# Another order for the first four chunks: scores of the second chunk ahead of the first y, six w_in pieces ahead of the third chunk's products

## The chip, the cores and the metric

The kernel runs on one core of a Trainium2 chip. The time is the device time of one execution in microseconds (us); before the change it is the median of three runs. Five engines work side by side, each through its own list of instructions in order: TensorE (PE, with its weight loads shown as PEld), VectorE (DVE), ScalarE (ACT), GpSimd (POOL) and SyncE (SP, which here issues the loads). They wait for each other through semaphores.

## The reference

A gated linear attention recurrence over 768 tokens (4 batches, 8 heads, 48 numbers a head) is followed by a feed-forward layer with SiLU on its 3072 rows of 384:

```python
for t in range(S):
    state = alpha[:, :, t, :, None] * state + np.einsum('bhd,bhe->bhde', k[:, :, t], v[:, :, t])
    y[:, :, t] = np.einsum('bhd,bhde->bhe', q[:, :, t], state)
x = y.transpose(0, 2, 1, 3).reshape(B * S, H * D)
h = x @ w_in                               # w_in 384 x 2048
out = (h * (1.0 / (1.0 + np.exp(-h)))) @ w_out   # w_out 2048 x 384
```

The weights w_in and w_out reach the kernel as 8-byte floats and are turned to 4-byte floats on the chip.

## The kernel before, in words

**Chunks.** The tokens are cut into 24 chunks of 128 (six for each batch; chunk n belongs to batch n mod 4). The recurrence of a chunk is done with matmuls. Four stages do it, each a function of the chunk's number:

- `products(n)`: PE transposes a (alpha), k and q; ACT copies a to SBUF (L731). DVE makes u, the products of alpha toward the chunk's end (a scan, L734), then kp = k times u (L745), then by `quotient(n)` the running products p (a scan, L764) and qp = q times p (L770). Below, these six DVE instructions are the chunk's DVE chain.
- `scores(n)`: PE multiplies kp with qp; ACT copies the two halves of the scores to g (L812), POOL sets what lies above the diagonal to zero (L813). PE transposes kp, and ACT copies that as kn (L832).
- `values(n)`: PE multiplies v with the masked scores (and the state with qp, from chunk 4 on), which is y; ACT copies y into `xt` (L863). One `xt` holds two chunks.
- `states(n)`: PE multiplies v with kn; ACT copies it as the state of a batch (L882), later DVE adds it.

**Feed-forward.** `enter_plain` multiplies an `xt` of two chunks with w_in, two tiles of 128 columns at a time: six matmuls and a SiLU on ACT (L923) are one step. `leave` multiplies with w_out. These steps stand in the list `pieces` and are dealt out between the stages by `fill`.

**Weights.** `weights` converts w_in in twelve pieces of 128 x 512 and then w_out in sixteen. For each piece ACT rounds the low words (`up`, L629) and DVE takes three instructions (L645, L646, L647). Raw bits lie in four buffers, and `fetch` loads the next piece once the buffer of the piece four before it has been read. `up` has two buffers. Pieces 0 to 2 are needed for the first four tiles of columns, 3 to 5 for the next four, and so on.

**Order.** The loop over `step` runs the four stages of neighbouring chunks, and after each stage (a slot) `fill` is called: up to `marks[0]`, at slot 10, it converts pieces of w_in (three of them), afterwards it gives out feed-forward steps as they fall due, with conversions ahead of them. Loads are issued in the same order on SP: `load(n)` brings a, k and q of a chunk, `load_v(n)` its v. Buffers for a, k and q exist twice, for kn and the scores g once, and PSUM has three banks (`ps_a`) in turn for transposes, scores, y and states. A planner orders the instructions of each engine unless they are held by `tc.keep_in_program_order`; `in_order` does that for PE's matmuls only from the time `late` is filled, some chunks further on. With both kernels the built program states each engine's list.

Of the kernel before, what the change touches and what calls it, by code (L numbers as in the profile page):

```python
# [8 lines left out]
F32 = mybir.dt.float32  # L9
# [4 lines left out]
ALU = mybir.AluOpType  # L14
# [341 lines left out]
def quotients(  # L356
# [22 lines left out]
    late = {}  # L379

    def in_order(ins):

        return tc.keep_in_program_order(ins) if late else ins

    class pe:
        @staticmethod
# [8 lines left out]
    C = 128  # L395
# [218 lines left out]
    def weights(which):  # L614

        pieces = [
            (w_in[:, t, c : c + 512], moe_w_in[t * 128 : t * 128 + 128, c : c + 512])  # L620
            for t, c in pieces_in
        ] if which == 0 else [
            (w_out[:, f, :], moe_w_out[f * 128 : f * 128 + 128, :]) for f in range(NFT)]
        def rounding(bits):
            n = bits.shape[1]
            up = upp.tile([128, 512], I32, name="up")[:, 0:n]

            tc.keep_in_program_order(
                act.activation(up, bits.bitcast(U32)[:, :, 0], AF.Copy, scale=2.0**-29))  # L629
            return up  # L630

        ahead = []
        for i, (dst, src) in enumerate(pieces):
            if not wide:
                act.dma_start(dst, src)
                yield
                continue
            assert which == 0 or conv_done[0] == n_conv[0]
            bits = coming.pop(0)
            up = ahead.pop() if ahead else rounding(bits)  # L640
            if which == i == 0:
                yield
            hi, w = bits[:, :, 1], dst.bitcast(I32)
            tc.keep_in_program_order(
                dve.tensor_scalar(w, hi, 3, 0x3FFFFFFF, ALU.logical_shift_left, ALU.bitwise_and))  # L645
            dve.scalar_tensor_tensor(w, hi, -(1 << 30), w, ALU.bitwise_and, ALU.bitwise_or)  # L646
            dve.tensor_tensor(w, w, up, ALU.add)  # L647
# [62 lines left out]
    def products(n):  # L710

        c = ctxs[n]
        sg = seg[0 if late else n % 2]
        ps = {}

        for name in ("a", "k", "q"):
            if n >= NA:
                if name == "a":
                    turned(c[name], tokens(sg))
                    load(n + 1, "a")  # L720
                continue
            if n < GB and name != "a":

                at = "kq".index(name)
                ps[name] = (bank(at) if n == 1 else out_bank(at, 512)).rearrange("p (j c) -> p j c", c=C)
            else:
                ps[name] = ps_attn()
            for j in range(NP):
                pe.transpose(ps[name][:, j, :], c[name][:, 2 * j : 2 * j + 2, :], ident)
            if name == "a":  # L730
                act.copy(tokens(sg), ps[name])  # L731
        end = NP * W
        u = upool.tile([128, end + 1], F32, name="u")
        dve.tensor_tensor_scan(u[:, end - 1 :: -1], sg[:, end:0:-1], one[:, end:0:-1],  # L734
                               0.0, ALU.mult, ALU.add)

        dve.tensor_single_scalar(least[:, n, :], u[:, 0:end:W], 2.0**-64, ALU.max)
        kp = c["kp"] = turns(kps, n) if n < NA else kps[0]
        ut = tokens(u)
        if n >= NA:  # L740
            ps["k"] = late["turn"].tile([128, NP, C], F32, name="turn")
            turned(c["k"], ps["k"])
            load(n + 1, "k")
        if n < NA:
            dve.tensor_tensor(kp, ps["k"], ut, ALU.mult)  # L745
            quotient(n, sg, ps["q"])
            return
        j = NP // 2
        dve.tensor_tensor(kp[:, 0:j], ps["k"][:, 0:j], ut[:, 0:j], ALU.mult)
        k, ut = [x[:, j:].rearrange("p j (e c) -> p j e c", e=2) for x in (ps["k"], ut)]  # L750
        dve.tensor_tensor(kp[:, j:].rearrange("p j (e c) -> p j e c", e=2)[:, :, ::-1], k, ut, ALU.mult)
        c["sg"] = sg

    def quotient(n, sg=None, q=None):

        c = ctxs[n]
        if sg is None:
            if n < NA:
                return
            sg = c.pop("sg")  # L760
        end, iv = NP * W, inv
        dve.reciprocal(iv[:, 0:end:W], least[:, n, :])
        p = turns(qps if n < NA else [qps[0], late["p"]], n)
        dve.tensor_tensor_scan(p[:, 0:end], sg[:, 0:end], iv[:, 0:end], 0.0, ALU.mult, ALU.add)  # L764
# [5 lines left out]
        dve.tensor_tensor(qp, q, qp, ALU.mult)  # L770

    def flip(n):

# [18 lines left out]
    def scores(n):  # L792
        c = ctxs[n]
        ci, b = c["ci"], c["b"]
        ps = [ps_attn() for _ in range(2)]

        for j in (0, 2, 1, 3):
            for e in range(2 if n >= NA else 1):  # L800
                for u in range(2):
                    r = slice(64 * u, 64 * u + D)
                    at = slice(CH * e, CH * e + CH) if n >= NA else slice(0, C)
                    t = slice(CH * (e ^ j // 2) if n >= NA else 0, C)
                    pe.matmul(ps[u][at, j, t], lhsT=c["kp"][r, j, at], rhs=c["qp"][r, j, t],
                              start=True, stop=True)
        g = decayed.rearrange("p (u j c) -> p u j c", u=2, j=NP)
        swapped = decayed.rearrange("p (o u j c) -> p o u j c", o=2, u=2, j=NP // 2)
        c["g"] = (lambda u, j: g[:, u, j, :]) if n < NA else (
            lambda u, j: swapped[:, j // 2, u, j % 2, :])  # L810
        for u in range(2 if n < NA else 0):
            act.copy(g[:, u], ps[u])  # L812
            gps.affine_select(g[:, u], g[:, u], pattern=[[0, NP], [1, C]], compare_op=ALU.is_ge,  # L813
                              fill=0.0, base=0, channel_multiplier=-1)
        if n >= NA:
            ps = [x.rearrange("p (o j) c -> p o j c", o=2) for x in ps]
            for u in range(2):
                act.copy(swapped[:, :, u, :, CH:], ps[u][:, :, :, CH:])  # L818
            for r, o in earlier:
                for u in range(2):  # L820
                    act.copy(swapped[r, o, u, :, 0:CH], ps[u][r, o, :, 0:CH])
            for at, half in ((CH, later), (0, earlier)):
                for r, o in half:
                    x = swapped[r, o].rearrange("p u j c -> p (u j) c")[:, :, at : at + CH]
                    gps.affine_select(x, x, pattern=[[0, NP], [1, CH]],  # L825
                                      compare_op=ALU.is_ge, fill=0.0, base=0, channel_multiplier=-1)
        if n < NA and ci < NCH - 1:
            ps_k = ps_attn()
            for j in range(NP):
                pe.transpose(ps_k[:, j, :], c["kp"][:, j, :], ident)  # L830
            c["kn"] = work.tile([128, NP, C], F32, name="kn")
            act.copy(c["kn"], ps_k)  # L832
        if ci > 0:
            s = st[b].rearrange("p j u e -> p j (u e)")
            for j in range(NP):
                mul = act.mul(s[:, j], s[:, j], least[:, n, j : j + 1])
                if late:
                    tc.keep_in_program_order(mul)
# [345 lines left out]
    def fill(step, slot):  # L1184

        at = step * SLOTS + slot
        if at < marks[0]:
            if at == SLOTS:
                next(conv[0])
            elif step >= 1:  # L1190
                convert(0, (at - SLOTS) * 3 // (marks[0] - SLOTS) + 1)
            return
        i = next(i for i, m in enumerate(marks[1:]) if at < m)
        a, b = [work_at[n] for n in ([0] + phases)[i : i + 2]]
        due = a + (b - a) * (at - marks[i] + 1) / (marks[i + 1] - marks[i])
        if at % 2 == 0 and step > 3 * GB + 2:
            next(audits, None)
        while work_at[done + 1] <= due and pieces[done][2] <= bridged:
# [2 lines left out]
            go_on()  # L1201

    for step in range(STEPS):
        if step == 1:
            load(NIN)
        stages = [[(scores, 1)], [(products, 0)], [(values, 1)], [(states, 1)]]
        if step == 1:

            stages = stages[1::-1] + stages[2:]
        elif step >= NA:  # L1210
            stages = [[(land, 1), (scores, 1)], [(products, 0)], [(quotient, 0)],
                      [(values, 1), (states, 1), (flip, 0)]]
        for slot, group in enumerate(stages):
            for stage, lag in group:
# [99 lines left out]
```

## Time and profile before

| | us |
|---|---|
| median of three runs | 557.77 (557.57 to 557.89) |
| the profiled execution | 557.26 |
| its span, first to last instruction | 555.5 |
| PE busy in the span | 541.4 |
| DVE busy in the span | 445.4 |
| ACT busy in the span | 208.5 |

The span is counted from the program's first instruction; a moment in the trace is given in us from there. A line of the timeline gives the start, the duration, the engine, the line of the kernel, the operation, what it writes and reads, and in square brackets the idle time before it and what ended it. Matmul counts in the trace are those of records: a 4-byte matmul of the program is mostly two of them.

### The profile page before, as it was taken

Reading aid. Unit: us, or ns where it says so; the run is one execution under the profiler, and the core shown is the slowest. Engines: PE = TensorE matmul, PEld = TensorE weight load, DVE = VectorE, ACT = ScalarE, POOL = GpSimd, SP = SyncE. Lnnn points to the kernel's source line nnn. Section 1 sums busy time; section 2 is a strip of 40 time slices with the busy share of each in tenths; the row PEclk is TensorE's granted clock in tenths of the full one; section 3 lists DMA queues with packets and bytes.
Section 4 is the critical chain, followed back from the end, with each engine's and each line's share of the span. In section 5 each row is a group of like instructions: output and inputs, shape, how many; then the busy total and the mean of one; then the engine's idle time right before and its main releaser. Section 6 shows DMA issues by size and latency. Waiting matters only on the chain. (4 is left out here: it accounts for less than half of the span.)

```text
span 555.5 us, 12640 instructions
## 1 busy us (share of the span) xinstructions
PE 541.4 (97%) x5026; PEld 489.7 (88%) x5026; DVE 445.4 (80%) x801; ACT 208.5 (38%) x466; POOL 76.1 (14%) x146
## 2 busy tenths in 40 slices
PE   6999999999999999999999999999999999999996
PEld 4788887998899999899999999988998999999996
DVE  5897788974999899997998986998884796945431
ACT  2556653223333253353353353344263342332100
POOL 3210000222210212021011021021121000001000
PEclk9999999999999999999999999999999999999999
DMA  9998971164454625355545654617642135500000
GB/s 215 246 249 210 232 195 33 47 161 116 117 136 125 159 63 138 86 145 149 139 112 139 193 139 120 191 27 183 170 137 91 54 91 169 172 11 22 10 24 30
DMA packets 99217, 70.09 MB, mean 126 GB/s; under 512 B 56272, under 2 KB 88656, under 8 KB 99152
## 3 DMA queue, kind: packets, MB, share of 16 engines
q1 hardware_dynamic: 97232, 65.30, 45.1%
q0 software_dynamic: 1920, 3.93, 2.0%
q8 instruction: 40, 0.66, 0.5%
q14 instruction: 25, 0.20, 0.1%
HBM read 61.34 MB, written 7.86 MB: 125 GB/s over the span
## 5 line engine op out<-in xcount | busy, mean ns | idle before, releaser
L388 PE MATMUL ps_o<-w_out,g 128*128 128x192 f32 x768 | 134.0, 328 | 0.5 <-DVE o L1056 0.5
L388 PEld LDWEIGHTS ps_o<-w_out,g 128*128 128x128 f32 x768 | 125.6, 190 | 3.5 <-DVE o L1056 1.0
L388 PE MATMUL ps_m<-xt,w_in 128*128 128x256 f32 x480 | 113.6, 383 | 1.5 <-ACT xt L863 1.1
L388 PEld LDWEIGHTS ps_m<-xt,w_in 128*128 128x128 f32 x480 | 89.1, 190 | 14.4 <-ACT xt L863 1.6
L388 PE MATMUL ps_o<-wt,g 128*128 128x192 f32 x576 | 99.7, 326 | 0.0
L388 PEld LDWEIGHTS ps_o<-wt,g 128*128 128x128 f32 x576 | 95.1, 190 | 1.6 <-issue 0.2
L388 PE MATMUL ps_m<-xc,w_in 128*128 128x256 f32 x288 | 70.7, 382 | 0.0
L388 PEld LDWEIGHTS ps_m<-xc,w_in 128*128 128x128 f32 x288 | 53.7, 190 | 7.0 <-DVE g L958 0.3
L1047 DVE TENSOR_TENSOR g<-g 128x512 f32<-128x512 f32 x72 | 50.1, 709 | 8.3 <-PE ps_o L388 8.3
L955 ACT ACTIVATE g<-g 128x1024 f32<-128x1024 f32 x32 | 33.1, 1056 | 61.2 <-DVE g L958 61.1
L1059 POOL DMA_DIRECT2D out_dram<-o x40 | 22.0, 551 | 219.5 <-DVE o L1056 113.7
L825 POOL TENSOR_SCALAR_AFFINE_SELECT g<-g 64x256 f32<-64x256 f32 x64 | 34.9, 546 | 124.4 <-ACT g L818 105.7
L388 PE MATMUL ps_m<-xc,wx 128*128 128x256 f32 x192 | 50.1, 383 | 1.0 <-DVE xc L586 1.0
L950 ACT COPY g<-ps_m 128x512 f32<-128x512 f32 x64 | 36.6, 588 | 37.0 <-PE ps_m L388 36.9
L388 PEld LDWEIGHTS ps_m<-xc,wx 128*128 128x128 f32 x192 | 35.2, 190 | 5.2 <-ACT u L1078 1.2
L958 DVE TENSOR_TENSOR g<-ps_m,g 128x512 f32<-128x512 f32 x56 | 37.1, 683 | 3.2 <-PE ps_m L388 2.7
L734 DVE TENSOR_TENSOR_SCAN u<-al,one 128x516 f32<-128x516 f32 x24 | 29.8, 1240 | 11.9 <-ACT al L731 11.6
L923 ACT ACTIVATE g<-ps_m 128x512 f32<-128x512 f32 x32 | 19.1, 597 | 41.7 <-PE ps_m L388 41.4
L950 ACT COPY part<-ps_m 128x512 f32<-128x512 f32 x32 | 18.9, 590 | 38.0 <-PE ps_m L388 24.0
L697 DVE TENSOR_REDUCE seen<-bits 128x1 f32<-128x512 int32 (+1 forms) x33 | 26.3, 823 | 5.7 <-DMA bits<-in_moe_w_in_dram 5.7
L764 DVE TENSOR_TENSOR_SCAN p<-al,inv 128x516 f32<-128x516 f32 x24 | 29.9, 1247 | 1.0 <-PE ps_a L388 0.3
L1056 DVE TENSOR_TENSOR o<-ps_o,u 128x192 f32<-128x192 f32 x24 | 8.5, 355 | 25.7 <-PE ps_o L388 22.8
(129 smaller groups left out, 648.5 us busy)
## 6 DMA issues: line engine op xcount, KB each, us to landing
bits<-in_moe_w_in_dram SPq DMA_DIRECT2D x24, 512.0 KB, 4.7
bits<-in_moe_w_out_dram SPq DMA_DIRECT2D x16, 384.0 KB, 3.9
at<-in_alpha_dram SPq DMA_DIRECT2D x64, 96.0 KB, 2.5
kt<-in_k_dram SPq DMA_DIRECT2D x64, 96.0 KB, 2.6
qt<-in_q_dram SPq DMA_DIRECT2D x64, 96.0 KB, 2.7
bits<-in_alpha_dram SPq DMA_DIRECT2D x9, 512.0 KB, 4.0
out_dram<-o POOLq DMA_DIRECT2D x40, 96.0 KB, 2.4
flips<-turn SPq DMA_DIRECT2D x12, 256.0 KB, 2.4
```

What stands on the lines that cost most here:

```text
L388: in_order(nc.tensor.matmul(*args, **kw))
L697: dve.tensor_reduce(seen[kind][which][:, i : i + 1], x, axis=AX, op=op, apply_absolute_value=True))
L734: dve.tensor_tensor_scan(u[:, end - 1 :: -1], sg[:, end:0:-1], one[:, end:0:-1], 0.0, ALU.mult, ALU.add)
L764: dve.tensor_tensor_scan(p[:, 0:end], sg[:, 0:end], iv[:, 0:end], 0.0, ALU.mult, ALU.add)
L825: gps.affine_select(x, x, pattern=[[0, NP], [1, CH]], compare_op=ALU.is_ge, fill=0.0, base=0, channel_multiplier=-1)
L923: act.activation(gts[grp, h, pair][:, i : i + 2, q % 2, :], ps, AF.Silu)
L950: act.copy(to, ps)
L955: act.activation(x, x, AF.Silu)
L958: dve.tensor_tensor(to, a, b, op)
L1047: dve.tensor_tensor(cells(grp, h, pair, *to), cells(grp, h, pair, *x), cells(grp, h, pair, *y), ALU.subtract)
L1056: dve.tensor_tensor(o, x, y, ALU.add)
L1059: (gps if grp < NG - 1 else nc.sync).dma_start(out[r : r + C, c * HO : (c + 1) * HO], o)
```

## The change

In `step` 1 the order of the stages becomes: products of chunk 1; scores of chunk 0; then scores of chunk 1 and values of chunk 0; states of chunk 0. In `step` 2 the slots hold nothing, values of chunk 1, states of chunk 1, products of chunk 2, so that the first feed-forward steps and the conversion of pieces 0 to 5 stand ahead of `products(2)`. The scores of chunk 1 and its kn get a place of their own, in one tile of the pool of g tiles. In the first four steps `settled` and `in_order` hold DVE's and PE's instructions in program order. The loads of chunks 2, 3 and 4 get new places among the slots (`load(NIN)`, `load(NIN + 1)`, `load(NIN + 2)` with NIN = 2).

```diff
     def in_order(ins):
-        return tc.keep_in_program_order(ins) if late else ins
+        return tc.keep_in_program_order(ins) if late or stated[0] else ins
+
+    stated = [True]
+
+    def settled(ins):
+
+        return tc.keep_in_program_order(ins) if stated[0] else ins
...
-            dve.scalar_tensor_tensor(w, hi, -(1 << 30), w, ALU.bitwise_and, ALU.bitwise_or)
-            dve.tensor_tensor(w, w, up, ALU.add)
+            settled(
+                dve.scalar_tensor_tensor(w, hi, -(1 << 30), w, ALU.bitwise_and, ALU.bitwise_or))
+            settled(dve.tensor_tensor(w, w, up, ALU.add))
...
-        dve.tensor_tensor(qp, q, qp, ALU.mult)
+        settled(dve.tensor_tensor(qp, q, qp, ALU.mult))
...
-        g = decayed.rearrange("p (u j c) -> p u j c", u=2, j=NP)
+        if n == 1:
+
+            room = gpool.tile([128, 4, 2, TB], F32, name="g").rearrange("p a b n -> p (a b n)")
+        g = (room[:, 0 : 2 * NP * C] if n == 1 else decayed).rearrange(
+            "p (u j c) -> p u j c", u=2, j=NP)
...
-            c["kn"] = work.tile([128, NP, C], F32, name="kn")
+            c["kn"] = room[:, 2 * NP * C :][:, 0 : NP * C].rearrange(
+                "p (j c) -> p j c", j=NP) if n == 1 else work.tile([128, NP, C], F32, name="kn")
...
             elif step >= 1:
-                convert(0, (at - SLOTS) * 3 // (marks[0] - SLOTS) + 1)
+                convert(0, 6 if at + 1 == marks[0] else (at - SLOTS) * 3 // (marks[0] - SLOTS) + 1)
+            if at == SLOTS + 2:
+                load(NIN)
+            if at + 1 == marks[0]:
+                load(NIN + 1)
             return
...
+        if at == 2 * SLOTS + 3:
+            load(NIN + 2)
+        if step == 2:
+            due = work_at[1 if at == marks[0] else 4]
...
     for step in range(STEPS):
-        if step == 1:
-            load(NIN)
+        stated[0] = step < 4
         stages = [[(scores, 1)], [(products, 0)], [(values, 1)], [(states, 1)]]
         if step == 1:
 
-            stages = stages[1::-1] + stages[2:]
+            stages = [[(products, 0)], [(scores, 1)], [(scores, 0), (values, 1)], [(states, 1)]]
+        elif step == 2:
+            stages = [[], [(values, 1)], [(states, 1)], [(products, 0)]]
...
-                if stage is states and n + 1 + NIN < NA:
+                if stage is states and NIN + 2 < n + 1 + NIN < NA:
                     load(n + 1 + NIN)
```

The other instructions of a chunk's DVE chain (u, least, kp, the reciprocal, p) are wrapped in `settled` in the same way. In the built programs the lists of PE, DVE and ACT differ up to the scores and the DVE chain of chunk 3 and are the same from there on, and SP's list is the same from the loads of chunk 4 on.

| order before | order after |
|---|---|
| PE: scores 0, values 0, states 0, scores 1, transposes of chunk 2 among values 1, states 1, w_in step, w_in step, scores 2, w_in step, transposes of chunk 3, w_in step, values 2 | PE: scores 0, scores 1, values 0, states 0, values 1, states 1, w_in step, transposes of chunk 2, three w_in steps, scores 2, transposes of chunk 3, values 2 |
| DVE: chains of chunks 0 and 1, pieces 0 to 2, chain of chunk 2, pieces 3 to 8 (the last inside the chain of chunk 3), pieces 9 to 11 | DVE: chains of chunks 0 and 1, pieces 0 to 5, chain of chunk 2, pieces 6 to 8, chain of chunk 3, pieces 9 to 11 |
| SP: a, k, q of chunk 2, w_in pieces 4 and 5, a, k, q of chunk 3, v of chunk 2, pieces 6 to 9 | SP: a of chunk 2, w_in pieces 4 and 5, k, q, v of chunk 2, pieces 6 to 9, a, k, q of chunk 3 |

More of the change, by code (lines that the diff above doesn't have):

```diff
@@ L733, in products @@
         u = upool.tile([128, end + 1], F32, name="u")
-        dve.tensor_tensor_scan(u[:, end - 1 :: -1], sg[:, end:0:-1], one[:, end:0:-1],
-                               0.0, ALU.mult, ALU.add)
-        dve.tensor_single_scalar(least[:, n, :], u[:, 0:end:W], 2.0**-64, ALU.max)
+        settled(dve.tensor_tensor_scan(u[:, end - 1 :: -1], sg[:, end:0:-1], one[:, end:0:-1],
+                                       0.0, ALU.mult, ALU.add))
+        settled(dve.tensor_single_scalar(least[:, n, :], u[:, 0:end:W], 2.0**-64, ALU.max))
         kp = c["kp"] = turns(kps, n) if n < NA else kps[0]
@@ L744, in products @@
         if n < NA:
-            dve.tensor_tensor(kp, ps["k"], ut, ALU.mult)
+            settled(dve.tensor_tensor(kp, ps["k"], ut, ALU.mult))
             quotient(n, sg, ps["q"])
@@ L761, in quotient @@
         end, iv = NP * W, inv
-        dve.reciprocal(iv[:, 0:end:W], least[:, n, :])
+        settled(dve.reciprocal(iv[:, 0:end:W], least[:, n, :]))
         p = turns(qps if n < NA else [qps[0], late["p"]], n)
-        dve.tensor_tensor_scan(p[:, 0:end], sg[:, 0:end], iv[:, 0:end], 0.0, ALU.mult, ALU.add)
+        settled(dve.tensor_tensor_scan(
+            p[:, 0:end], sg[:, 0:end], iv[:, 0:end], 0.0, ALU.mult, ALU.add))
         qp = c["qp"] = tokens(p)
```

## The prediction

> **What bounds the kernel now.** I read the page's busy shares first, then busy time by stretch, then the timeline of the first 50 us engine by engine, and the waits last; the chain that ended last names only the final store and is no help.
>
> ```profile
> PE 541.4 (97%) x5026; PEld 489.7 (88%) x5026; DVE 445.4 (80%) x801; ACT 208.5 (38%) x466; POOL 76.1 (14%) x146
> ...
> 4.20:24.26 20.06, 18.58 (x203) 13.78 (x203) 15.66 (x26) 8.76 (x18) 4.18 (x8) 1.00 1.22 263
> 24.26:38.21 13.95, 13.95 (x82) 11.63 (x83) 12.88 (x22) 7.96 (x15) 1.67 (x2) 1.00 0.89 226
> 38.21:49.45 11.24, 11.24 (x121) 9.30 (x121) 8.84 (x15) 5.65 (x11) 1.22 (x2) 1.00 0.81 245
> ```
>
> After each stretch and its length the columns are busy time of PE, PEld, DVE, ACT and POOL. From 24.26 us PE is never idle, so the change can gain only what PE loses before, in waits and in slow matmuls, and keeps only what later stretches do not take back. All that is changed lies before about 50 us.
>
> ```profile
> 10.02 1.12 PE L392 MATMUL ps_m<-ident,qn 128*128 128x128 f32 x4
> 11.06 2.08 PE L388 MATMUL ps_a<-p,kp 48*128 48x128 f32 x16
> 13.07 1.12 PE L392 MATMUL ps_a<-ident,kp 128*128 128x128 f32 x4
> ...
> 17.77 1.47 PE L388 MATMUL ps_a<-p,kp 48*128 48x128 f32 x16
> 19.17 0.66 PE L392 MATMUL ps_a<-ident,kp 128*128 128x128 f32 x4
> ...
> 24.26 1.99 PE L388 MATMUL ps_m<-xt,w_in 128*128 128x256 f32 x8 [0.26 <-ACT xt L863]
> ...
> 45.27 1.16 PE L388 MATMUL ps_a<-p,kp 48*128 48x128 f32 x16
> 46.37 0.66 PE L392 MATMUL ps_a<-ident,kp 128*128 128x128 f32 x4
> 46.86 2.75 PE L388 MATMUL ps_m<-xt,w_in 128*128 128x256 f32 x12
> ```
>
> Columns: start, duration, engine and so on. The same scores take 2.08, 1.47 and 1.16 us: PE's clock rises between 17.8 and 19.2 us (the clock row shows full speed from the start; the durations decide). The first w_in product starts at 24.26, 0.05 after the copy of chunk 1's y.
>
> ```profile
> 13.67 0.69 DVE L770 TENSOR_TENSOR p<-ps_m,p 128x512 f32<-128x512 f32 x1
> 14.28 0.46 DVE L645 TENSOR_SCALAR w_in<-bits 128x512 int32<-128x512 int32 x1
> 14.77 1.00 DVE L646 SCALAR_TENSOR_TENSOR w_in<-bits,w_in 128x512 int32<-128x512 int32 x1
> ...
> 21.97 1.23 DVE L734 TENSOR_TENSOR_SCAN u<-al,one 128x516 f32<-128x516 f32 x1 [1.57 <-ACT al L731]
> ...
> 46.80 0.69 DVE L647 CUSTOM_DVE_ANT_0 w_in<-w_in,up 128x1024 uint16<-128x1024 uint16 x1
> 50.76 1.23 DVE L734 TENSOR_TENSOR_SCAN u<-al,one 128x516 f32<-128x516 f32 x1 [3.26 <-ACT al L731]
> ```
>
> DVE converts w_in in twelve pieces and makes a chunk's kp and qp between them, almost without rest until 47.49, when piece 11 is done. The product that starts at 46.86 needs piece 11 for its third matmul, at 46.86 + 2 x 0.465 = 47.79: only 0.3 us of slack. So two engines bound this stretch, PE and close behind it DVE.
>
> **The skill.** "TensorE: Matmul & The Clock Gate", Part 1, says the clock doubles after about 3.4 us of sustained matmuls; Part 4 says transposes do not count as such activity. The trace agrees with the second: transposes fill PE from 4.22 to 11 and nothing speeds up; the rise comes after the matmuls that run from 14.5. The forecast goes by it, with the trace's durations.
>
> **The change part by part.** The instructions stay the same in kind and number; only their order, two buffers and the places of loads change. Unit costs from the trace: four transposes 0.97 us to the next issue on the slow clock, 0.44 on the fast; scores of a chunk 2.01 and 1.10; y of a chunk (values) about 1.7 and 1.0; one step of w_in products, six matmuls, 2.79 (39.22 to 42.01), so 0.465 a matmul; a piece on DVE 1.89 (18.42 less 16.52); a chunk's DVE chain 4.17 (21.97 to 26.14). ACT, back to back: y copy 0.37, rounding 0.57, state copies 0.6, a score copy 0.55, silu 0.5. A semaphore 0.05 to 0.1.
>
> *Scores of chunk 1 ahead of y of chunk 0.* They wait for DVE's qp of chunk 1 (13.67 + 0.69 = 14.36), so PE is as before until 14.2, and then runs: scores 14.42, kp transpose 16.43, y of chunk 0 17.40, its states, y of chunk 1, its states. No PE wait for the triangle mask is left (two of 0.3 before): POOL masks chunk 0 while PE scores chunk 1. Mask and k-transpose of chunk 1 need their own buffers, else they would wait for chunk 0's readers; the change takes one of the six g tiles for them. The next five tiles fit without a wait and the ring is six again: cost nothing.
>
> *When the y of chunk 1 is copied* depends on the clock. If it rises at 18.4: y of chunk 0 ends at 19.0; ACT copies it 19.05, then in its new order rounds (19.42), copies states (19.99), rounds (20.57) and only then copies y of chunk 1, 21.14 to 21.62. If the clock stays low until about 21.8 (scores and transposes now stand where y and states stood in the window that raised it): y of chunk 1 ends at 21.87, copy 21.92 to 22.40. So w_in products start at 21.67 or at 22.45, against 24.26. But before, PE had by then chunk 2's three groups of transposes behind it (3 x 0.44 = 1.33), and 0.2 of states still ahead. The real lead is 24.26 - 21.67 - 1.33 + 0.2 = 1.46, or 0.68.
>
> *Six pieces ahead of chunk 2's chain, stated order on DVE.* DVE loses its 1.57 wait. Pieces from 14.3: six by 1.89, 0.3 each for two that run beside POOL's masks (L646 took 1.00 instead of 0.69), 0.15 for a rounding: piece 2 ends 20.9, in time for the first product; piece 5 at 26.4; chunk 2's chain 26.4 to 30.57; pieces 6, 7, 8 end at 32.4, 34.3, 36.2. PE now does four w_in steps and the transposes before chunk 2's scores: start + 4 x 2.79 + 1.33 = 34.14 or 34.92. The chain at 30.57 is hidden there by more than 3 us.
>
> *Loads.* Chunk 2's a keeps its place (issued 11.43); k and q are moved behind two w_in pieces that wait for buffers (DVE's L646 ends at 15.8 and 17.7), so they issue near 18.2 and 19.5. Landings in a full queue stand 1.2 us apart for 192 KB and 1.35 for 512 KB, so k lands near 22.5 and q 23.7, needed at 24.9 and 25.3. Chunk 3's a, k, q move behind four more pieces: last of them near 33, needed at 36. Nothing; cover 1.5 us at the least. Below nothing is excluded, as no load holds this stretch before.
>
> *What is late next.* (a) Before, 2.79 of products stood between chunk 2's scores and chunk 3's transposes; now these follow at once, and a's needs the buffer that ACT's first score copy frees. Scores end at 34.14 + 1.16 = 35.30; on ACT ahead of the copy stand a rounding that waits for piece 7 (34.3) and a silu, so copy 35.45 to 36.0, transposes 36.05 to 37.37 instead of 35.7 to 37.0. (b) y of chunk 2 needs both masks, POOL 36.1 to 37.6. It ends, to the next issue, at 38.55; before it was 39.22. Lead 0.67. With the low clock the same sum gives 39.15, lead 0.07. (c) Chunk 3's a is copied at 37.6 (38.2) instead of 35.5, and DVE, in stated order, waits for it: 37.65 + 4.17, then pieces 9 to 11 in 5.65: 47.4 (48.0). The third matmul of the product after chunk 3's scores starts at 47.5 (48.1) against 47.79.
>
> Sum: 0.3 us gained, or 0.3 lost. From there on all engines keep the old order and PE the difference. Against the profiled execution's own 557.26 (span 555.5 and 1.76 around it) that is 556.96 or 557.56; the median of the runs is 557.77, 0.5 above that execution, so 557.47 or 558.07. The two are about equally likely; I forecast the middle, no change, 557.7. From no change this kernel's measurement tells 0.2%, or 1.1 us.
>
> **Rivals.**
> *The whole lead stays* (faster). If DVE did not wait in (c) and ACT not in (a), the lead of 1.46 would hold: 556.3. For: DVE's work from 14.3 is 12 x 1.89 + 2 x 4.17 + 0.67 = 31.7, ending at 46.0 with no wait. Against: the chain scores, copy, transpose, copy, scan is one of true dependences.
> *The clock rises a window later still* (slower). Products then start at 22.45 on the slow clock, and up to 25.3 half of that time is lost: 1.4 more beside the 0.3, so 559.5. It decides from a start of the products, counted at full clock, of about 23.3. For: PE's four transposes at 16.43 break the run of matmuls. Against: from 17.4 y, states, y, states give over 4 us without a break.
> *Nothing moves* in effect: y of chunk 1 is so late on ACT that PE starts near 22.0; then leads cancel exactly and 557.8 stands.
>
> **How the numbers follow.** Forecast with its two branches 0.60 (own range 557.1 to 558.4), nothing moves 0.13, whole lead 0.12, late clock 0.15. Faster by over 0.2% (under 556.65): most of the whole lead, 0.11. Slower by over 0.2%: most of the late clock and some mishap on the loads, 0.16. The rest, 0.73, is within. The range takes in most of the lead and of the late clock: 556.5 to 559.2.
>
> **What would show it.** Right: products from 21.6 to 22.5; the DVE wait of 1.57 gone and one of about 1 us ahead of chunk 3's scan; a PE wait for ACT at chunk 3's a; piece 11 at 47.4 to 48.0; chunk 4's transposes within 0.4 us of 49.45. Wrong: transposes that still take 1.1 us after 22; a wait for k or q of chunk 2 or 3; piece 11 before 47; or a difference that arises after 50 us, where the order is the old one.

## The result

The changed kernel takes 558.31 us (median of 22 runs, 557.65 to 559.30); the kernel before, in the same rounds, 557.35 (22 runs, 555.95 to 558.23). The ratio is 1.0023, with a 95% interval of 1.0017 to 1.0029: slower by 0.23%, some 1.3 us (the two medians lie 0.96 apart). No change was forecast (557.7, a gain or loss of 0.3 at most). That 558.31 still lies in the predicted range is partly luck: in these rounds the kernel before took 557.35, not the 557.77 from which the forecast started. The profiled execution took 558.79 with a span of 557.1.

The page's busy shares and the busy time by stretch of the changed kernel (columns as before; the stretches end where w_in's products start and where chunk 3's and chunk 4's transposes start):

```profile
PE 541.3 (97%) x5026; PEld 490.1 (88%) x5026; DVE 447.1 (80%) x801; ACT 208.9 (37%) x466; POOL 77.6 (14%) x146
```

```profile
4.11:22.31 18.20, 16.51 (x192) 12.88 (x192) 15.12 (x23) 8.49 (x17) 4.77 (x8) 1.00 1.13 265
22.31:36.53 14.22, 13.62 (x80) 11.70 (x81) 12.61 (x23) 7.54 (x15) 0.00 (x0) 1.00 1.00 247
36.53:50.17 13.64, 13.31 (x133) 10.66 (x133) 11.17 (x17) 6.56 (x13) 3.82 (x4) 1.00 0.72 214
```

PE's busy time is the same to 0.1 us; DVE's has grown by 1.7 and POOL's by 1.5, with the same number of instructions on each. And PE, which before was busy in every microsecond from its first product on, is not any more (14.22 and 13.62, 13.64 and 13.31). Its timeline:

```profile
16.41 1.12 PE L398 MATMUL ps_a<-ident,kp 128*128 128x128 f32 x4
17.45 1.93 PE L394 MATMUL ps_a<-g,vn 128*32 128x128 f32 x32
...
22.31 2.86 PE L394 MATMUL ps_m<-xt,w_in 128*128 128x256 f32 x12 [0.96 <-ACT xt L876]
25.01 0.60 PE L398 MATMUL ps_a<-ident,an 128*128 128x128 f32 x4
...
36.53 0.66 PE L398 MATMUL ps_a<-ident,an 128*128 128x128 f32 x4 [0.60 <-ACT g L824]
...
38.73 1.07 PE L394 MATMUL ps_a<-g,vn 128*32 128x128 f32 x28 [0.33 <-POOL g L825]
39.73 2.86 PE L394 MATMUL ps_m<-xt,w_in 128*128 128x256 f32 x12
...
47.37 2.96 PE L394 MATMUL ps_m<-xt,w_in 128*128 128x256 f32 x12
50.17 0.60 PE L398 MATMUL ps_a<-ident,an 128*128 128x128 f32 x4
```

The products start at 22.31, 1.95 earlier than in the profile of before. Chunk 4's transposes, from which on PE's list is the old one, start at 50.17 in place of 49.45, 0.72 later. Two waits at chunk 3 are new, 0.60 and 0.33. A third does not show in brackets: the step at 47.37 takes 2.96, where the same step took 2.75 before (at 46.86). Its third matmul waits 0.10 for piece 11, and the record after that wait needs 0.32 to the next one instead of 0.22. VectorE in the same stretch:

```profile
14.68 1.00 DVE L653 SCALAR_TENSOR_TENSOR w_in<-bits,w_in 128x512 int32<-128x512 int32 x1
...
17.71 0.90 DVE L654 CUSTOM_DVE_ANT_0 w_in<-w_in,up 128x1024 uint16<-128x1024 uint16 x1
18.53 0.85 DVE L651 TENSOR_SCALAR w_in<-bits 128x512 int32<-128x512 int32 x1
...
26.85 1.23 DVE L741 TENSOR_TENSOR_SCAN u<-al,one 128x516 f32<-128x516 f32 x1
...
36.45 0.69 DVE L654 CUSTOM_DVE_ANT_0 w_in<-w_in,up 128x1024 uint16<-128x1024 uint16 x1 [0.59 <-ACT g L936]
37.06 1.12 DVE L1046 TENSOR_TENSOR g<-g 128x512 f32<-128x512 f32 x1
38.10 1.66 DVE L741 TENSOR_TENSOR_SCAN u<-al,one 128x516 f32<-128x516 f32 x1
...
47.59 0.69 DVE L654 CUSTOM_DVE_ANT_0 w_in<-w_in,up 128x1024 uint16<-128x1024 uint16 x1
51.48 1.23 DVE L741 TENSOR_TENSOR_SCAN u<-al,one 128x516 f32<-128x516 f32 x1 [3.19 <-ACT al L738]
```

The wait of 1.57 ahead of chunk 2's scan is gone, as the change means it to be. But operations have grown: 0.69 to 0.90, 0.42 to 0.85, 0.68 to 1.12, and the scan of chunk 3 takes 1.66 where that of chunk 2 takes 1.23. The last conversion, piece 11, ends at 48.28 in place of 47.50. Beside each grown operation stands a pair of masks on POOL. First before, then after:

```profile
19.98 1.50 POOL L813 TENSOR_SCALAR_AFFINE_SELECT g<-g 128x512 f32<-128x512 f32 x2 [4.75 <-ACT g L812]
31.93 1.67 POOL L813 TENSOR_SCALAR_AFFINE_SELECT g<-g 128x512 f32<-128x512 f32 x2 [10.46 <-ACT g L812]
```

```profile
17.13 1.98 POOL L825 TENSOR_SCALAR_AFFINE_SELECT g<-g 128x512 f32<-128x512 f32 x2 [1.99 <-ACT g L824]
36.55 2.13 POOL L825 TENSOR_SCALAR_AFFINE_SELECT g<-g 128x512 f32<-128x512 f32 x2 [17.44 <-ACT g L824]
```

Before, the masks of chunk 1 ran from 19.98 to 21.47, while VectorE waited for chunk 2's a (20.4 to 21.97). Now they run from 17.13 to 19.11, beside conversions. A mask by itself takes 0.63, and up to 1.10 beside VectorE's work.

The times show that the two engines take turns here. The masks of chunk 2 one by one (VectorE's sum at 37.06 and scan at 38.10, shown above, start beside the first and the second):

```profile
36.55 1.09 POOL L825 TENSOR_SCALAR_AFFINE_SELECT g<-g 128x512 f32<-128x512 f32 x1 [17.44 <-ACT g L824]
37.59 1.09 POOL L825 TENSOR_SCALAR_AFFINE_SELECT g<-g 128x512 f32<-128x512 f32 x1
```

In the order mask, sum, mask, scan each ends as if it ran its own time (0.63, 0.68, 0.63, 1.23) from 0.14 before the end of the other engine's operation ahead of it. The first mask stands behind the conversion that ends at 37.14: 37.14 - 0.14 + 0.63 = 37.63, and the trace has 37.64. By the same sum the others end at 38.18, 38.67 and 39.77; the trace has 38.18, 38.68 and 39.76. In the sixteen profiles 164 operations between 13 and 52 us start while one of the other engine's runs, and all end by this sum within 0.02 us. VectorE's product qp, with one input in PSUM, is the exception: it and a mask overlap 18 times, and neither holds the other. So the growth is waiting for the other's turn, and a forecast could have summed it: the profile of before has such turns too, as in the conversion of 1.00 at 14.77.

### The profile page after: what moved, and what is told of

The parts are those of the page before. It is cut to its first block, busy times and chain, and to the rows that moved or that the text cites. A ratio compares the mean times of both kernels' runs of the same rounds, so it can differ in the third digit from the quotient of the medians.

```text
span 557.1 us, 12636 instructions
## 1 busy us (share of the span) xinstructions
PE 541.3 (97%) x5026; PEld 490.1 (88%) x5026; DVE 447.1 (80%) x801; ACT 208.9 (37%) x466; POOL 77.6 (14%) x146
```

## The experiments

In the expectations, theory A is that PE's new waits at chunk 3 set the end, B that the clock and PE's order at the start do, C that ScalarE's queue does (the copy of the scores stands behind a rounding that waits for VectorE), and D, formed after the first four runs, that VectorE's piece 11 does.

**One half of the reordering at a time.** Both kernels have the stated order. The first keeps the order of scores, y and states and leaves the conversion, the loads and chunk 2's products as before:

```diff
-convert(0, 6 if at + 1 == marks[0] else (at - SLOTS) * 3 // (marks[0] - SLOTS) + 1)
+convert(0, (at - SLOTS) * 3 // (marks[0] - SLOTS) + 1)
...
-            stages = [[], [(values, 1)], [(states, 1)], [(products, 0)]]
+            stages = [[], [(products, 0)], [(values, 1)], [(states, 1)]]
```

> One part alone: scores of the second chunk ahead of the first y, with their own buffers, and DVE and PE in stated order; conversion, loads and the third chunk's products stay where they were before. Theory A (the loss is the dependence at the fourth chunk: its transposes and the third chunk's y come right behind the third chunk's scores, and wait for ACT's copy, 0.60 us, and POOL's mask, 0.33): nothing of that kind here, so within 0.3 us of the kernel before. Theory B (the loss is PE's clock and order at the start: y of both chunks on the slow clock): slower than before by 0.5 to 0.8 us here too.

The second keeps the pieces and loads, and puts scores 1 back behind y of chunk 0, without buffers of their own:

```diff
-            stages = [[(products, 0)], [(scores, 1)], [(scores, 0), (values, 1)], [(states, 1)]]
+            stages = stages[1::-1] + stages[2:]
...
-            stages = [[], [(values, 1)], [(states, 1)], [(products, 0)]]
+            stages = [[(scores, 1)], [(values, 1)], [(states, 1)], [(products, 0)]]
```

> The other part alone: first and second chunk in the order of before, but six pieces and three w_in steps ahead of the third chunk's products and scores, with the new places of the loads and the stated order. Theory A: the transposes of chunk 3 (counted from 0) again come right behind scores 2 and wait; products start near 23 instead of 22.3, so slower than before by 1.2 to 1.8 us. Theory B: the clock rises at 18 to 19 as before, so no slower than before.

Measured: the first 558.86, ratio 1.0022 (1.0009 to 1.0035); the second 559.55, ratio 1.0040 (1.0023 to 1.0057). Each half is slow by itself, the second by its median more than the whole. The first half has none of the new waits at chunk 3; PE waits for conversions instead, 0.51 at 31.79 and 1.04 at 48.33. That does not fit A. B's 0.5 to 0.8 would fit the first within its interval, but B had the second no slower than before, so it falls as well.

**Taking PE's waits at chunk 3 away.** One step of products is moved between the transposes of kp of chunk 2 and those of chunk 3; in the second kernel the roundings of pieces 6 and later are also issued one step later:

```diff
-            due = work_at[1 if at == marks[0] else 4]
+            due = work_at[1 if at == marks[0] else 3]
+        if at == 3 * SLOTS:
+            due = work_at[4]
```

```diff
-            convert(0, 3 * (done // 2) + 6)
+            convert(0, 3 * ((done - 1) // 2) + 6 if done else 6)
```

> The changed kernel, with one of the four w_in steps moved from ahead of scores 2 to between kp's transposes and those of chunk 3. ACT's copy of the scores still stands behind a rounding that waits for DVE's piece 7 (34.8). Theory A as plain distance on PE: the waits of 0.60 and 0.33 go and the time is 0.9 us under the changed kernel. Theory C (what holds the copy is ACT's queue behind DVE): the copy starts near 35.5 instead of 35.9, and only about 0.4 us is won.

> The same, and the roundings of pieces 7 to 9 behind the score copies of chunk 2 on ACT, so that the copy waits for PE alone (near 33). Theory C: y of chunk 2 ends 1.5 us sooner than in the changed kernel, and what is then late is piece 11, near 47.1 against 48.3: 1.0 to 1.2 us under the changed kernel, 0.2 to 0.5 under the kernel before. Theory A: the same as the run before it. Theory B: still 0.5 slower than the kernel before.

Measured: 558.48, ratio 1.0018 (1.0011 to 1.0025), and 559.33, ratio 1.0032 (1.0022 to 1.0042). The list of what PE waited for between the first product and chunk 4's transposes; the columns are us in total, times, longest. First the changed kernel, then the one with the step between:

```profile
PE ps_m L394 <- ACT xt L876: 1.0, 1, 1.0
PE ps_a L398 <- ACT g L824: 0.6, 1, 0.6
PE ps_a L394 <- POOL g L825: 0.3, 1, 0.3
```

```profile
PE ps_m L394 <- ACT xt L876: 1.1, 1, 1.1
PE ps_m L394 <- DVE w_in L654: 0.7, 1, 0.7
```

Both waits at chunk 3 are off this list (0.12 of the first is left in the timeline), and y of chunk 2 is done 0.8 earlier (38.92 in place of 39.73). A wait of 0.75 for a conversion takes their place:

```profile
48.34 1.99 PE L394 MATMUL ps_m<-xt,w_in 128*128 128x256 f32 x8 [0.75 <-DVE w_in L654]
50.17 0.60 PE L398 MATMUL ps_a<-ident,an 128*128 128x128 f32 x4
```

Piece 11 ends at 48.28 as in the changed kernel, and chunk 4's transposes start at 50.17, to the hundredth where they were. A falls as the whole cause: what PE is given ahead of piece 11 it gives back there. With later roundings y is earlier still (38.27), but piece 7 waits 1.06 for its rounding, piece 11 ends at 48.91, and the total rises with it. C, which had 1.0 to 1.2 us under the changed kernel here, falls too.

**The masks.** The masks of chunks 1 and 2 are left out of both kernels:

```diff
-            gps.affine_select(g[:, u], g[:, u], pattern=[[0, NP], [1, C]], compare_op=ALU.is_ge,
+            if n not in (1, 2):
+                gps.affine_select(g[:, u], g[:, u], pattern=[[0, NP], [1, C]], compare_op=ALU.is_ge,
```

> The changed kernel without GpSimd's two pairs of masks for chunks 1 and 2 (so it leaves out the causal masking of these chunks' scores and its results differ). Theory D (VectorE sets the end of this stretch: its piece 11 is late because the masks now run beside its conversions and lengthen them, 1.8 us of lengthened operations, of which some 1.2 go with these two pairs): VectorE's operations at 17-19 and 36-38 us keep the length they have elsewhere (0.69, 0.42, 0.68, 1.23), piece 11 ends 1.0 to 1.2 earlier (47.1 to 47.3), chunk 4's transposes start near 49.1, and the total is 0.8 to 1.1 under the changed kernel. Theory A (the new waits of the matmul engine for ScalarE and GpSimd at chunk 3 set the end): GpSimd's 0.33 of wait goes, total 0.3 lower. Theory C (ScalarE's queue): no change.

> The control: the kernel before without the same two pairs of masks (so it leaves out the causal masking of chunks 1 and 2). There the pair of chunk 1 lies at 20 us where VectorE waits for data, and only the pair of chunk 2 lies beside VectorE's work (0.3 to 0.6 of lengthening). Theory D: 0.3 to 0.6 under the kernel before, so clearly less than what the changed kernel gains by the same edit. Theory A: what y waits for GpSimd goes in both, 0.3. If both gain the same, the masks do not explain the difference between the two kernels.

Measured: 558.02, ratio 1.0012 (1.0005 to 1.0019), and 557.22, ratio 0.9994 (0.9985 to 1.0004). In the changed kernel piece 11 ends at 47.13, 1.15 earlier, and chunk 4's transposes start at 49.02, as D said:

```profile
47.19 1.99 PE L394 MATMUL ps_m<-xt,w_in 128*128 128x256 f32 x8 [0.52 <-DVE w_in L654]
49.02 0.60 PE L398 MATMUL ps_a<-ident,an 128*128 128x128 f32 x4
```

PE's wait of 0.33 for a mask goes with the same edit, but the wait of 0.52 for piece 11 shows what PE now waits for last. From chunk 2's scan to the end of piece 11 the kernel before gains 0.29 (25.53 to 25.24); its total is not to be told apart from the kernel before, where D had 0.3 to 0.6. The total of the changed kernel falls by 0.11% (0.02% to 0.20%, from the two intervals), 0.6 us, at the low side of D's 0.8 to 1.1. So the masks are a part of it; without them the changed kernel is still the slower one.

**The stated order alone,** with stages, loads and conversions as in the kernel before (VectorE's instructions are wrapped in `settled` as in the change):

```diff
     def in_order(ins):
-        return tc.keep_in_program_order(ins) if late else ins
+        return tc.keep_in_program_order(ins) if late or stated[0] else ins
...
     for step in range(STEPS):
+        stated[0] = step < 4
```

> The kernel before with the stated order of TensorE and VectorE alone: order of stages, loads and conversions as before. In the kernel before the planner lays piece 8 and one of the side-by-side sums between the dependent operations of chunk 3's scan chain (35.97 to 41.92 for work that takes some 6.65 one after another). Theory D: with the stated order these run one after another, piece 11 ends 0.6 to 0.8 later (48.1 to 48.3) and the total is 0.5 to 0.8 above the kernel before. Theories A and C (the cost is in the order of the stages): no change against before, within 0.2.

Measured: 558.09, ratio 1.0016 (1.0008 to 1.0024), so 0.9 us with no reordering of stages at all; D had 0.5 to 0.8. VectorE in the kernel before, then in this one, at chunk 3's chain:

```profile
36.30 1.23 DVE L734 TENSOR_TENSOR_SCAN u<-al,one 128x516 f32<-128x516 f32 x1
37.44 0.67 DVE L646 SCALAR_TENSOR_TENSOR w_in<-bits,w_in 128x512 int32<-128x512 int32 x1
38.03 0.16 DVE L737 TENSOR_SCALAR least<-u 128x4 f32<-128x4 f32 x1
```

```profile
38.10 1.23 DVE L741 TENSOR_TENSOR_SCAN u<-al,one 128x516 f32<-128x516 f32 x1
39.37 0.17 DVE L744 TENSOR_SCALAR least<-u 128x4 f32<-128x4 f32 x1
```

The planner had laid a conversion between the scan and the operation that needs its result. An independent operation starts 0.1 before the one ahead of it ends (37.44 against 36.30 + 1.23), a dependent one after it, here by 0.04. From chunk 2's scan to the end of piece 11 this kernel takes 26.52 (22.02 to 48.54), the kernel before 25.53. Of the 1.0, 0.63 is what operations beside masks have grown by more than before, the lost interleaving the other 0.4. The larger part is thus masks again: this cost and that of the masks can't be added.

**The start of the products.** In the changed kernel one conversion fewer is asked for ahead of the y of chunk 1, so that ScalarE copies y before it rounds:

```diff
-convert(0, 6 if at + 1 == marks[0] else (at - SLOTS) * 3 // (marks[0] - SLOTS) + 1)
+convert(0, 6 if at + 1 == marks[0] else min(2, (at - SLOTS) * 3 // (marks[0] - SLOTS) + 1))
```

> The changed kernel with ScalarE's copy of chunk 1's y put ahead of one rounding (one piece less is converted ahead of chunk 2's chain at that point), so that the first w_in products start 0.7 earlier, at 21.6 instead of 22.31. Theory A (the matmul engine's lead decides): the total falls by 0.5 to 0.7. Theory D (VectorE's piece 11 decides): the lead is given back as a wait of the products for a conversion, and the total stays within 0.2 of the changed kernel.

Measured: 558.35, ratio 1.0016 (1.0008 to 1.0024), from the changed kernel not to be told apart. In its profile the products start at 20.98, 1.33 earlier than in the changed kernel's; PE then waits 1.45 for chunk 3's first transposes, and chunk 4's start at 49.68. That is 0.49 earlier, and piece 11 is 0.48 earlier (47.80), 0.31 of it because VectorE's wait for a rounding at 20.56 is gone. Of PE's lead only what VectorE gained too is kept: against A, for D. (A part of the lead is the clock's, which rose earlier in this profile: y of chunk 0 took 1.44 in place of 1.93.)

**A second profile of each kernel,** unchanged.

> The kernel before, unchanged, for a second profile: how far one execution's numbers can be trusted. [...]piece 11's end moves by at most 0.3 from 47.50, because VectorE's idle 1.57 ahead of chunk 2's scan is what the clock changes. If the profiles of one kernel agree within 0.1 everywhere, the difference of 0.7 at 50 us and the difference of 1.5 at the end are both the change's.

> The changed kernel, unchanged, for a second profile, with the same question: piece 11 at 48.28 within 0.3 and chunk 4's transposes at 50.17 within 0.3, whatever the clock does, if VectorE sets the end there; the remaining 0.8 of the 1.5 at the end, which came in steps at 219 and 402 us, is chance if it differs between the two profiles by 0.3 or more.

The two profiles of the changed kernel agree to 0.03 in the start of the products, in piece 11 (48.28, 48.29) and in chunk 4's transposes (50.17, 50.18). Those of the kernel before do not. Timelines of PE, the first profile and the second:

```profile
16.83 1.01 PE L388 MATMUL ps_a<-vn,kn 128*32 128x48 f32 x25
17.77 1.47 PE L388 MATMUL ps_a<-p,kp 48*128 48x128 f32 x16
```

```profile
16.91 0.59 PE L388 MATMUL ps_a<-vn,kn 128*32 128x48 f32 x25
17.43 1.47 PE L388 MATMUL ps_a<-p,kp 48*128 48x128 f32 x16
...
23.65 1.56 PE L388 MATMUL ps_m<-xt,w_in 128*128 128x256 f32 x6 [0.26 <-ACT xt L863]
...
48.85 0.60 PE L392 MATMUL ps_a<-ident,an 128*128 128x128 f32 x4
```

The clock rose earlier, at 16.8 in place of 18.4 by the durations of single records: the same states take 0.59 in place of 1.01. (The scores behind them take 1.47 both times: in the second profile at the full clock, but with the first records 0.2 to 0.3 apart.) The products start at 23.65 in place of 24.26, and chunk 4's transposes at 48.85 in place of 49.45. VectorE's wait ahead of chunk 2's scan is 0.73, not 1.57. The expectation that piece 11 would move by 0.3 at most was wrong: it moved by 0.57, to 46.93. Between 381 and 405 us the second profile loses 0.73 against the first with the same instructions, so the end of one profile can't be trusted to less than that; the stretch up to 50 us can. The changed kernel's two spans differ by 0.5 (557.1 and 556.6), which by its expectation makes the rest of the 1.5 chance.

**The side-by-side sum.** To shorten VectorE's list and nothing else, the first side-by-side sum (0.67 us), which the planner draws ahead into chunk 3's chain, is held at its place in the program, and in a second pair of kernels put right behind piece 11:

```diff
-        dve.tensor_tensor(x, x, cells(grp, h, pair, 1, 1), ALU.add)
+        ins = dve.tensor_tensor(x, x, cells(grp, h, pair, 1, 1), ALU.add)
+        if grp == h == pair == 0:
+            tc.keep_in_program_order(ins)
```

```diff
-            side_by_side(0, i % 2, i // 2)
+            if i:
+                side_by_side(0, i % 2, i // 2)
...
             convert(0, 3 * (done // 2) + 6)
+            if done == 4:
+                tc.keep_in_program_order(side_by_side(0, 0, 0))
```

> The kernel before with one edit: the first side-by-side sum (0.67 us on VectorE, at 40.2 us), which the planner had pulled ahead into the scan chain of chunk 3, keeps its place in the program some tens of microseconds later. Theory D (VectorE's piece 11 sets the end of this stretch): piece 11 ends 0.5 to 0.7 earlier, near 46.9, chunk 4's transposes start near 48.9, and the total is 0.3 to 0.7 under the kernel before, unless the later place costs it back. Theory A (the matmul engine's waits at chunk 3): no change, within 0.2.

> The same edit on the changed kernel, where this sum stands at 37.06 us between piece 8 and chunk 3's scan and takes 1.12 us beside the masks. Chunk 3's a is copied only at 37.94 there, so VectorE can start the scan no earlier than 37.95 in place of 38.10. Theory D with this floor: piece 11 at most 0.2 to 0.4 earlier and the total 0.1 to 0.4 under the changed kernel, less than the same edit gives the kernel before. Theory D without it: 1.1 earlier. Theory A: no change.

> The kernel before with the first side-by-side sum put right behind piece 11, where VectorE has idle time ahead of chunk 4's scan; nothing else differs. Theory D: from the start of chunk 2's scan to piece 11's end 25.2 in place of 25.5 (as with the sum still later), and, since the sum no longer stands in the way at 105 to 126 us, this 0.3 reaches the end: 0.2 to 0.5 under the kernel before. If VectorE does not set the end there: no change, within 0.15.

> The same edit on the changed kernel: piece 11 at 47.96 and chunk 4's transposes at 49.84, as with the sum still later (0.34 earlier than 50.18), and no loss at 105 to 126 us: 0.3 under the changed kernel, so about 1.0018 to 1.0024 against the kernel before in place of 1.0023 to 1.0029. If VectorE does not set the end: no change against the changed kernel.

Held at its place it gave 1.0011 (1.0001 to 1.0021) on the kernel before and 1.0029 (1.0017 to 1.0041) on the changed one. That decides nothing, since between 101 and 127 us, where the sum now stands, the two profiles lose 0.34 and 0.53. Right behind piece 11 it gave 1.0000 (0.9990 to 1.0011) on the kernel before, which misses D's 0.2 to 0.5, and 1.0016 (1.0010 to 1.0023) on the changed one, 0.4 us less than the change, with intervals that overlap. The traces are clearer. On the kernel before VectorE's stretch falls by the 0.3 (25.21 from chunk 2's scan to piece 11), and PE from its first product to chunk 4's transposes takes 25.19 as ever. On the changed kernel those transposes follow piece 11, to 49.84 and 49.46. PE's wait of 0.33 for a mask goes there too, since the mask no longer waits for the sum's turn, so this pair alone would not tell PE's limit from VectorE's.

**All profiles together,** in us; PE's idle time is from the first product on, in gaps over 0.1.

| kernel | products start | PE idle | piece 11 ends | chunk 4's transposes | from piece 11 to them | from first product to them |
|---|---|---|---|---|---|---|
| before | 24.26 | 0 | 47.50 | 49.45 | 1.95 | 25.19 |
| before, second profile | 23.65 | 0 | 46.93 | 48.85 | 1.91 | 25.19 |
| before, no masks | 23.68 | 0 | 46.84 | 48.87 | 2.02 | 25.19 |
| before, sum held | 24.34 | 0 | 47.53 | 49.53 | 2.00 | 25.19 |
| before, sum behind piece 11 | 23.78 | 0 | 46.87 | 48.97 | 2.10 | 25.19 |
| after | 22.31 | 0.93 | 48.28 | 50.17 | 1.88 | 27.86 |
| after, second profile | 22.34 | 0.92 | 48.29 | 50.18 | 1.89 | 27.83 |
| scores only | 22.38 | 1.70 | 48.27 | 50.16 | 1.89 | 27.77 |
| pieces only | 23.51 | 0.40 | 49.40 | 51.29 | 1.89 | 27.78 |
| step between | 22.44 | 0.87 | 48.28 | 50.17 | 1.89 | 27.73 |
| step between, later roundings | 22.39 | 1.71 | 48.91 | 50.80 | 1.88 | 28.40 |
| stated order only | 23.21 | 1.27 | 48.54 | 50.43 | 1.89 | 27.22 |
| y first | 20.98 | 1.78 | 47.80 | 49.68 | 1.89 | 28.70 |
| after, no masks | 20.26 | 1.68 | 47.13 | 49.02 | 1.89 | 28.76 |
| after, sum held | 22.48 | 0.57 | 47.96 | 49.84 | 1.88 | 27.36 |
| after, sum behind piece 11 | 22.00 | 0.66 | 47.57 | 49.46 | 1.89 | 27.45 |

Two constants split the kernels. With the order of before, chunk 4's transposes come 25.19 after the first product, whatever is done to VectorE: PE is the bound and has no gap. With the stated order, alone or with any part of the change, they come 1.88 or 1.89 after piece 11, a semaphore of 0.05 and four matmuls of 1.83 together, whatever is done to PE: VectorE's piece 11 is what PE waits for last.

In six of these eleven profiles (the changed kernel's two, pieces only, y first, and the two with the sum moved) that last wait is only 0.10, too short for the table. In the changed kernel PE's own list is close behind: from y of chunk 2 to chunk 4's transposes it is the old one and takes 10.23 (39.22 to 49.45 before), so from 39.73 PE would have come to 49.96 by itself. Both limits hang on VectorE, since the copy of the scores stands behind a rounding that waits for piece 7, and the masks wait for VectorE's turns.

The change moved the stretch from the first limit to the second, and the second lies higher: 50.18 against 49.13, the mean of the five rows of before. This 1.05 lies within the 0.95 to 1.6 that the ratio gives.

## Why the prediction was wrong

*The start* was right in its number: products from 21.67 or 22.45, measured 22.31; VectorE's wait of 1.57 gone; no wait of PE or VectorE for a load. The clock took neither branch (18.4 or 21.8): single records quicken at 20.1 in both profiles. Chunk 1's y, done at 21.0, was copied at 21.78 behind ScalarE's roundings, as in the first branch. PE's work to chunk 4's transposes from there is 25.19 + 1.31 for chunk 2's transposes - 0.20 for states, so they could have started at 48.61: a lead of 0.84, where 0.68 or 1.46 was predicted.

*Steps (a) and (b),* the chain at chunk 3, were right in kind and too small. On ScalarE:

```profile
34.83 0.69 ACT L635 ACTIVATE up<-bits 128x512 int32<-128x512 uint32 x1 [0.73 <-DVE w_in L654]
...
35.90 1.07 ACT L824 COPY g<-ps_a 128x512 f32<-128x512 f32 x2
...
37.32 0.62 ACT L738 COPY al<-ps_a 128x512 f32<-128x512 f32 x1
```

The copy of the scores began at 35.90, not 35.45, behind a rounding that waited 0.73 for piece 7 (34.80, not 34.3). The masks took 2.13, not 1.5. The y of chunk 2 was done at 39.73, not 38.55 or 39.15, and before it was 39.22: where a lead of 0.67 or 0.07 was summed, PE was 0.51 behind. That is 0.51 of the 0.72 at chunk 4's transposes; piece 11 adds 0.21. But the kernel with the step between shows that mending this alone gains nothing: piece 11 then holds PE until the same 50.17.

*Step (c) is the one that failed,* in its premise. It let VectorE stand ready at chunk 3's scan and wait about 1 us for a, so that piece 11 followed from PE's time. Chunk 3's a was copied by 37.94, inside the predicted 37.6 to 38.2, and there was no wait: VectorE was busy until then, and the scan began at 38.10. Piece 8 was put at 36.2 and ended at 37.14. The terms: 0.6 was allowed for growth beside the masks and 0.95 came up to there; 0.15 was allowed for a rounding and 0.31 came (20.56, where 20.25 is the usual distance); and 0.45 of delay ahead of piece 8's last operation was not foreseen. Then the side-by-side sum stood in front of the scan, 0.68 of work that (c) left out and that took 1.12, and the scan itself grew by 0.43. Piece 11 was put at 47.4 or 48.0 and came at 48.28. The slack was taken as 0.3 and was 0.17: in the profile of before the third matmul starts at 47.72, 0.22 after piece 11 (the prediction took 0.465 a matmul, and in this step it is 0.43), and the semaphore takes 0.05 of that. So VectorE, taken as the one that waits, was the one that is waited for.

*The stated order was costed at nothing* ("the instructions stay the same in kind and number"). In the kernel before it costs 1.0 on VectorE and 0.9 of the total by itself. The rival that kept the whole lead summed VectorE's work to 31.7 us from 14.3. It took 34.1: in the second profiles of the two kernels VectorE needs 34.08 against 32.56 from the first piece to piece 11's end. Of these 1.52, 0.98 are grown operations, 0.29 idle time, and 0.25 overlap that dependent operations in a row don't have.

*The base.* The sum was made against one profile of before, with its clock late (a wait of 1.57). In the five profiles with that order of PE the first product starts at 23.94 in the mean, 0.3 earlier than in the one used. So a part of the lead was that execution's own. This also ends the forecast's two branches for the clock: in the kernel before the clock's phase reaches the end through VectorE's wait and PE's start, in the changed one hardly, because VectorE has pieces to convert meanwhile.

*After 50 us* nothing can be laid to the change: the profile's span shows 1.5 in all, but the kernel before differs by 0.73 from itself there.

Of the Trainium skill, "TensorE: Matmul & The Clock Gate", Part 1, names a free-running window as the reason why the moment of the rise varies, by 0.5 us either way. The two profiles of before agree that it varies, as the same states at 16.9 us ran at either speed, but by more, 16.8 against 18.4; the window itself is not in these traces. "SBUF — State Buffer", the section "Who interferes with whom", says that VectorE operations with two SBUF inputs contend with a GpSimd instruction that reads SBUF, and that the one that issues second is blocked until the first is done. The traces agree: conversions with two SBUF inputs (0.69 to 0.90 and 1.00), the sum (0.68 to 1.12) and the scan (1.23 to 1.66) took turns with the masks by the sum shown above, and qp, with one input in PSUM, did not. That both sides grew is no contradiction, because each in turn was the second. The conversion with one input took turns too (0.42 to 0.85); for such an operation the page names a mode that uses the shared ports, and which mode ran the traces do not tell.

Left open: why piece 8's last operation starts 0.45 late. Its rounding had ended 2.8 us before, and in every kernel with the pieces moved ahead, also without masks, it starts 1.27 to 1.28 after the operation ahead of it; with only the scores moved or only the order stated it is 0.83. The total gained less without masks than the trace says. And the changed stages with VectorE's order left to the planner were not run, so what the reordering is worth without the stated order is not known.

## What to carry to other kernels

Give the slack of the second engine as a number, from the last thing that it hands over to the point where the bound engine needs it, and follow a gained microsecond on both; here PE's lead of 0.84 met a list on VectorE with 0.17 of slack. An order fixed by hand keeps the instructions and loses what a planner had laid between dependent operations, so price it from the trace, operation by operation. Filling an engine's idle time with its own later work gains less where that time had sheltered another engine's traffic: in the first profile of before the masks of chunk 1 ran in VectorE's wait, and once the wait was filled the two engines had to take turns. Such turns can be summed beforehand.

## What the runs showed of the hardware

- A mask of 128 x 512 takes GpSimd 0.63 us alone and up to 1.10 beside VectorE in these two kernels, and VectorE's operations beside it took longer too (0.42 to 0.85, 0.69 to 1.00, 0.68 to 1.12, 1.23 to 1.66). They take turns: the one that starts second runs its own time from 0.14 before the end of the first, within 0.02 us in 164 cases. Beside VectorE's qp, with one input in PSUM, neither waited (18 cases).
- An operation on VectorE that needs the result of the one before it starts after its end, by 0.04 at 39.37 in the kernel with the stated order alone and by 0.14 at 47.59 in the changed one; an independent one starts about 0.1 before that end. Between chunk 2's scan and piece 11 the lost interleaving came to 0.4 us.
- From one record of w_in's matmuls to the next it is 0.22 us in a run of them and 0.32 just behind a wait, so that a wait of 0.10 for piece 11 cost PE 0.21.
- The rise of TensorE's clock differs between executions of one kernel: the same 25 records took 1.01 and 0.59 us at 16.9 us, and the products that follow moved by 0.61.
